# A convolution and feed-forward kernel on one Trainium2 core: the weight sums of two groups move from Pool to VectorE, and the first blocks' list is written anew

## The chip, the core and the metric

The kernel runs on one core of a Trainium2 chip. The metric is the time of one execution in microseconds (us) on the device; less is better. The engines have these names here: TensorE (PE in the profile; its weight loads are PEld), VectorE (DVE), ScalarE (ACT), Pool (GpSimd, POOL) and SyncE (SP, which here only issues transfers). Each engine works through its own list of instructions in order; between engines, semaphores make one wait for another.

## The reference

All data are float32. Each of 32768 tokens (8 sequences of 4096) has 192 channels in 8 heads of 24. First a causal convolution with 7 taps, softmaxed per head, then a feed-forward layer:

```python
w = softmax(weight, axis=-1)                          # 8 heads x 7 taps
out = np.einsum('hk,bskhg->bshg', w, x_unf)           # x_unf: 7 shifted views of x, zeros in front
h = out.reshape(B * S, 192) @ w_in                    # 192 x 2048
g = h * (1.0 / (1.0 + np.exp(-h)))
return g @ w_out                                      # 2048 x 192
```

## The kernel before, in words

**Blocks.** The tokens are taken in 32 blocks of 1024, as two halves of 512. A block is loaded (`load`, L184), turned by VectorE so that channels lie on partitions (`turn_in`, L474, "i"), given the 6 columns ahead of it (`halo_in`, L489, "ha": a small copy, then a transfer on SP's queue), convolved (`conv`, L502, "v": tap 0 by ScalarE; taps 1 to 6 by VectorE for the blocks up to 3, later by ScalarE and accumulating transfers), copied by SP's queue into the slots that the products read (`spread`, L523, "sp"), and six combinations of the slots are made by VectorE (`win`, L537, "w").

**Products.** Block 0 uses the plain products (`up_plain`, L577, and `down_plain`, L777, whose matmuls stand in 48 steps "dp"). All later blocks use a scheme of the Strassen kind with fewer products. For it the weights of five groups g = 0 to 4 are replaced in place by sums of each other: `combine(g, e)` (L379), with e = 0 for partitions 0 to 63 of the tiles and e = 1 for 64 to 127. `combine` makes 8 sums for e = 0 and 11 for e = 1, each on 64 partitions by 128 columns, from two operands in SBUF (group 4's first half has 3 more). Groups 0, 4 and 1 are combined by Pool at the end of the preparation (L1087), groups 2 and 3 by a step "go" of the list (L920): Pool copies one element of the loaded block, which makes it wait for that load, and then makes the 38 sums. Behind them on Pool stand the 16 sums for the output weights (`combine_out`, L417, 128x192 each), which `down_plain` issues with its last step.

**A block from 1 on.** Products P (`product`, L635; two matmul records each in the trace), six plain steps L (`plain`, L659), ScalarE's copies u of partial sums out of PSUM, VectorE's sums X, a, b (`sums_h`, L686), ScalarE's activations S and SL; then VectorE's differences t of the activations (`sum_g`, L718), the output products D (`out_slot`, L735), and the merging M, x, y, z, the transposes o and stores st. Step P13.0 reads a PSUM bank that X2.0 has written, P11.0 one of X4.0; P2 and P3 read window 1, P6 and P9 window 0. P2.0 accumulates into the bank that u5.0 has to copy first.

**The order.** Every engine's order is the order of the list: PLAN (L81) for blocks from 3 on, START (L104) for the first blocks. A step's mark tells the block: "=" two back, "-" one back, "+" one ahead of the pass; in START "=v.21" is tap 1 of channel group 2 for block 1, "-P5.0" a product of block 1, and unmarked steps belong to block 2 (a load, tap, spread or window is for the block after the one that the mark names). `step` (L882) turns a mark into instructions, all pinned in program order. A step's place matters only against steps of the same engine or queue; data and buffers (PSUM banks by the tables CHAIN_BANKS, XBANKS, PLAIN_BANKS and ACC) do the rest. In START of before the windows of block 1 stand behind all 18 VectorE taps of block 1, its 3 transposes for block 2 follow those taps, and taps of block 2 fill the gaps between the sums.

Of the kernel before, what the change touches and what calls it, by code (L numbers as in the profile page):

```python
# [12 lines left out]
ALU = mybir.AluOpType  # L13
# [4 lines left out]
def kernel(  # L18
# [83 lines left out]
        "u0.3 P9.3 S2.3 S0.4"  # L102
    )
    START = (  # L104
        "-ld.1 =v.10 -ld.0 =v.00 =v.11 =v.12 =dp.0 =dp.1 =dp.2 =dp.3 =v.13 =v.20 =v.21 =v.22 "
        "=v.23 =v.24 =v.25 =dp.4 =dp.5 =v.14 =dp.6 =dp.7 =dp.8 =dp.9 =v.15 =v.16 -ld.2 =sp.1 "
        "=dp.10 =dp.11 =v.26 =v.01 =v.02 =v.03 =dp.12 =v.04 =dp.13 =v.05 =v.06 =dp.14 =dp.15 "
        "=dp.16 =sp.2 =dp.17 =dp.18 =dp.19 =dp.20 =sp.0 -i.2 =go.2 -i.1 =dp.21 =dp.22 =dp.23 "
        "=dp.24 -i.0 =dp.25 =dp.26 =dp.27 =dp.28 =dp.29 =dp.30 -ha.0 =dp.31 =dp.32 =dp.33 "
        "=dp.34 ld.1 =w.0 =w.1 =dp.35 =dp.36 -v.00 =dp.37 =dp.38 =w.2 =dp.39 =dp.40 =dp.41 "  # L110
        "-v.01 =dp.42 -v.20 =dp.43 =dp.44 -v.02 -v.03 -v.10 -v.11 -v.12 =dp.45 =cp.0 =dp.46 "
        "=dp.47 =cp.1 -v.21 -P5.0 =w.3 -P5.4 -L.00 -u5.0 -v.13 -v.14 -L.11 -v.22 -P2.0 =cp.2 "
        "-u5.4 -P2.4 -L.12 -P3.0 -u4.0 -u4.4 -P6.0 -L.02 -u2.0 -L.01 -SL.0 -L.10 -SL.1 -P6.4 "
        "-u2.4 -P3.4 -SL.2 =o.1 -v.15 -P1.0 -u0.0 -X2.0 -P13.0 -S2.0 -v.23 -P5.2 =w.4 -u5.2 "
        "-P9.0 -P1.4 -u0.4 -P0.0 -u1.0 -P12.0 -P2.2 -X2.4 -P0.4 -P13.4 -S2.4 -X4.0 -P7.0 -u1.4 "
        "=o.2 -P14.0 -b1.0 -P10.0 =w.5 -S3.0 -u4.2 -a5.0 -b5.0 -S5.0 -v.04 -P11.0 -P9.4 -X4.4 "
        "-P14.4 =o.0 -P4.0 -S4.0 -a1.0 -P6.2 -u2.2 -P5.1 -P12.4 -b1.4 -P11.4 -P7.4 -P3.2 -P1.2 "
        "-P8.0 -u5.1 -S4.4 -a5.4 -P10.4 -u0.2 -S3.4 -P2.1 -u4.1 -P4.4 =st.0 -X2.2 -P13.2 -S2.2 "
        "-P9.2 -P0.2 -u1.2 -a0.0 -b5.4 -S5.4 -a1.4 -P12.2 -v.16 -P6.1 -u2.1 =st.1 -P5.3 -u5.3 "
        "-P8.4 -P14.2 -X4.2 -S3.2 i.1 -a0.4 -b1.2 -P3.1 -X2.1 -P1.1 -P7.2 -u0.1 -a5.2 -P2.3 "  # L120
        "-u4.3 -P3.3 -P11.2 -v.24 -P9.1 -S4.2 -X4.1 -P13.1 -P4.2 -P6.3 -S2.1 -a1.2 -u2.3 -P10.2 "
        "-b5.2 -P0.1 -P7.1 -P8.2 -P11.1 -X2.3 -P1.3 -S1.0 -P9.3 -v.25 -u1.1 -P14.1 -S4.1 -P12.1 "
        "-u0.3 -S1.4 -P13.3 -S3.1 -a5.1 -P4.1 -X4.3 -P7.3 -P0.3 -a0.2 -S5.2 -sp.1 +ld.1 -P12.3 "
        "P5.4 -v.26 -P11.3 -b1.1 -a5.3 -a1.1 -u1.3 -P10.1 -b1.3 -S2.3 -P4.3 -a1.3 -v.05 =st.2 "
        "-P8.1 -b5.1 -P10.3 -sp.2 -S0.4 -P14.3 -P8.3 ld.0 -S4.3 -S1.1 P5.0 -a0.1 -S0.0 -t.00 "
        "-D1.31 -D1.11 -S0.2 -D1.01 -S3.3 -D1.30 -t.01 -D2.00 -D2.01 -b5.3 -S5.3 -S1.2 -S5.1 "
        "-D0.11 -t.03 -D4.00 -a0.3 -D4.01 -t.02 -D3.00 u5.4 -D0.20 -S0.1 ld.2 -D5.00 -t.10 "
        "-t.11 -D2.11 -D3.01 -v.06 -sp.0 -D1.20 -S0.3 -D5.01 -t.13 -D4.11 -D5.10 -D4.10 i.2 "
        "-S1.3 i.0 -t.12 -D5.11 -D3.11 -t.20 ha.0 -t.21 -D0.10 -D2.10 u5.0 -D2.21 -w.0 -D2.20 "
        "-w.1 v.20 -D3.10 -D0.00 v.00 -t.23 -D4.21 -D4.20 -w.2 v.01 -t.22 -D3.21 -D0.21 -D0.30 "  # L130
        "-D0.31 -w.3 -t.30 v.21 -t.31 -D1.10 v.02 v.22 -D0.01 -D2.31 -t.32 -t.33 -D1.21 v.10 "
        "-D5.30 v.23 v.24 -y0.0 -D1.00 -y1.0 -D5.31 -z1.0 -D5.20 -D5.21 -x2.0 -x2.2 v.11 -D3.31 "
        "-D2.30 -x2.1 v.03 -x2.3 P2.0 u4.0 P3.0 -w.5 L.02 P2.4 u4.4 v.12 v.13 v.14 P6.0 u2.0 "
        "v.15 v.25 v.26 v.04 -M1.0 -M2.0 -y2.0 L.00 +ld.0 -M6.0 L.01 SL.0 X2.0 P6.4 u2.4 -D4.30 "
        "-D3.20 -D3.30 -M3.0 -x0.0 -D4.31 -x1.0 P9.0 P1.0 u0.0 -o.0 P13.0 S2.0 X4.0 P1.4 u0.4 "
        "-M4.0 -M5.0 P3.4 P5.1 u5.1 P11.0 X2.4 -w.4 P7.0 S4.0 P0.0 P12.0 P2.1 u1.0 P9.4 P0.4 "
        "u1.4 P13.4 a5.0 P4.0 b1.0 P10.0 X4.4 u4.1 S2.4 P7.4 P11.4 S4.4 P14.4 S3.4 v.16 P6.1 "
        "u2.1 P14.0 v.05 L.10 a1.0 a5.4 +ld.2 b5.0 P8.0 +i.2 a0.0 S3.0 P3.1 P4.4 a1.4 L.11 L.12 "
        "SL.1 P5.2 P12.4 SL.2 X2.1 v.06 P8.4 -st.0 u5.2 P1.1 P13.1 u0.1 b1.4 P5.3 sp.1 S0.0 "
        "u5.3 -o.3 S2.1 P12.1 P2.2 u4.2 -M7.0 P9.1 P0.1 u1.1 S1.4 +i.1 P2.3 u4.3 +i.0 a0.4 X4.1 "  # L140
        "S0.4 P10.4 P6.2 u2.2 P3.2 P7.1 P14.1 S3.1 P11.1 b1.1 b5.4 +ha.0 P10.1 +v.20 S4.1 P3.3 "
        "-o.1 P6.3 u2.3 X2.2 P9.2 P1.2 u0.2 a5.1 P4.1 X2.3 +v.21 P13.2 S2.2 P13.3 S2.3 P1.3 "
        "u0.3 -st.1 +v.00 P9.3 b5.1"
    )
    QUEUE = (0, 4, 1, 2, 3)
    CHAIN_BANKS = (
        ((4, 1, 2, 7, 7), (3, 4, 6, 5, 5), (1, 3, 3, 1, 0)),
        ((0, 2, 5, 4, 6), (1, 6, 1, 0, 7), (5, 3, 2, 3, 0)),
        ((5, 2, 5, 6, 7), (0, 4, 0, 3, 3), (1, 7, 2, 1, 1)),
    )  # L150
    XBANKS = (
        ((6, 2, 4, 2, 0), (6, 0, 0, 0, 4)),
        ((5, 1, 2, 7, 3), (4, 7, 3, 7, 4)),
        ((4, 0, 1, 7, 4), (6, 3, 1, 7, 6)),
    )
    PLAIN_BANKS = (
        (0, 2, 1),
        (5, 3, 4),
        (6, 3, 1),
    )  # L160
    ACC = (
        (1, 2, 7, 4, 3, 5, 7),
        (3, 4, 6, 1, 0, 2, 7),
        (0, 6, 1, 3, 4, 2, 7),
    )

# [10 lines left out]
    vec, act = Pinned(nc.vector), Pinned(nc.scalar)  # L177
# [4 lines left out]
    nats, xts, gs = {}, {}, {}  # L182
# [23 lines left out]
    x0 = x.flatten_outer_dims()[TB - pad : TB, :].rearrange("t (k c) -> c k t", k=NK)  # L206
# [11 lines left out]
    warm = const.tile([P, 1], F32, name="warm")  # L218
# [9 lines left out]
    pool = Pinned(nc.gpsimd)  # L228
# [138 lines left out]
            q >= NJ // 2,  # L367
        )

    def comb(out, u, v, op):  # L370
        pool.tensor_tensor(out, u, v, op=op)

    PLAIN = (1, NJ - 1, 1)

    def raw(g, i, k, e):
        a, j, own = chunks(g)[i]
        return rows(wr[j] if own == e else ws[j], e)[:, a, k, :]

    def combine(g, e):  # L379

        def op(sign, to, u, v):
            comb(raw(g, *to, e), raw(g, *u, e), raw(g, *v, e), ALU.add if sign > 0 else ALU.subtract)

        if (g, e) == (SWAP[0], 0):
            op(-1, (2, 1), (1, 0), (1, 2))
            op(-1, (2, 1), (2, 1), (0, 0))
            op(-1, (2, 1), (2, 1), (0, 1))
        for order in COMBINE[e]:
            op(*order)
# [382 lines left out]
                )  # L772
            )

    DOWN_BANKS = (0, 1, 5)

    def down_plain(b):  # L777

# [103 lines left out]
    def step(b, token):  # L882

        if token[0] in BACK:
            b, token = b - BACK[token[0]], token[1:]
        name, arg = token.split(".") if "." in token else ("", "")
        if b < 0 or b >= NB or not name or (b, token) in did:
            return
        if b == NB - 1 and token in held:
            return  # L890
        if b == NB - 1 and token[:3] == "D3." and (b, closing) not in did:
            later.append(token)
            return
        did.add((b, token))
        digits = [int(c) for c in arg]
        if name[0] == "P":
            product(b, digits[0], int(name[1:]), *digits[1:])
        elif name == "L":
            plain(b, *digits)
        elif name == "SL":  # L900
            silu_plain(b, *digits)
        elif name[0] in "uXabS":
            sums_h(b, name, *digits)
        elif name == "t":
            sum_g(b, *digits)
        elif name[0] == "D":
            i, (j, e) = int(name[1]), digits
            for half in range(2) if i == 3 and b == NB - 1 else (None,):
                out_slot(b, j, i, e, half)
        elif name[0] in "Mzyx":  # L910
            merge(b, name, *digits)
        elif name == "o":
            turn_out(b, *digits)
        elif name == "st":
            store_out(b, *digits)
        elif name == "dp":
            next(downs)
        elif name == "cp":
            copy_plain(b, *digits)
        elif name == "go":  # L920
            pool.tensor_copy(warm, nats[1][:, digits[0], 0, 0:1])
            for g in (2, 3):
                for e in range(2):
                    combine(g, e)
        elif name == "ld":
            if b + 1 < NB:
                load(b + 1, digits)
        elif b + 1 < NB:
            {"i": turn_in, "ha": halo_in, "v": conv, "sp": spread, "w": win}[name](
                b + 1, *digits[: 1 + (name == "v")]  # L930
            )
        if b == NB - 1 and token == closing:
            for t in later:
                step(b, t)
# [200 lines left out]
```

## Time and profile before

| | us |
|---|---|
| median of 3 runs (2319.98 to 2320.62) | 2320.21 |
| the profiled execution | 2319.66 |
| its span, first to last instruction | 2318.0 |
| TensorE busy in the span | 2309.5 |
| VectorE busy | 1797.6 |
| ScalarE busy | 1496.6 |
| Pool busy | 530.8 |

The profiled execution was taken from first to last instruction; 1.7 us of its time lie around the span. The granted TensorE clock was 0.999. The stages at the start, from the answer on stretches (busy us in each; start and end in us from the span's start):

| stretch | what TensorE does | PE | DVE | ACT | POOL |
|---|---|---|---|---|---|
| 0 to 59.67 | convolution and block 0, first layer | 58.19 | 52.44 | 29.84 | 25.23 |
| 59.67 to 101.02 | block 0, second layer | 41.35 | 39.90 | 9.42 | 39.39 |
| 101.02 to 137.95 | block 1, products | 36.93 | 33.69 | 28.28 | 26.97 |
| 137.95 to 178.03 | block 1, outputs (16 records of block 2 between) | 40.08 | 38.97 | 12.31 | 0.00 |
| 178.03 to 209.69 | block 2, products | 31.66 | 28.98 | 26.74 | 1.89 |
| 209.69 to 245.90 | block 2, outputs | 36.21 | 27.08 | 19.16 | 13.07 |

How to read the profile: a group or timeline line has the engine, the line of the kernel, the operation, the tile written and the tiles read, the shapes, and how many; what stands in brackets is the time that the engine sat idle before it and what ended that. Instructions of one engine overlap a little, so that the distance from one start to the next is often shorter than a duration. Matmul ends are modelled: TensorE counts as busy in stretches where its matmuls run at a poorer pace, and starts have to be compared.

### The profile page before, as it was taken

How to read it: one execution, taken by the hardware profiler on the slowest of the kernel's cores; microseconds unless marked ns; L12 is line 12 of the kernel's file. 1: busy time of each engine (PE TensorE's matmuls, PEld its weight loads, DVE VectorE, ACT ScalarE, POOL GpSimd, SP SyncE). 2: the span in 40 equal slices, each digit the busy share in tenths (PEclk: the TensorE clock that was granted, in tenths of full speed). 3: DMA queues.
4: the chain of work that ended last, by engine and by line, in shares of the span. 5: the costliest groups of instructions: out<-in, count | busy, mean ns of one | idle time of the engine just before them, and what ended most of it. 6: DMA issues, size and time to landing. Idle time of an engine off the chain costs nothing.

```text
span 2318.0 us, 45422 instructions
## 1 busy us (share of the span) xinstructions
PE 2309.5 (100%) x17630; PEld 950.3 (41%) x17630; DVE 1797.6 (78%) x2373; ACT 1496.6 (65%) x2779; POOL 530.8 (23%) x672
## 2 busy tenths in 40 slices
PE   9999999999999999999999999999999999999998
PEld 5454443444433344433444333443334443344433
DVE  8998777777777777777777777777778777777777
ACT  5347766677666686666776666866667666677543
POOL 4921112221122211222212222112221212221100
PEclk9999999999999999999999999999999999999999
DMA  7236556765567765677655676656676557765401
GB/s 159 58 62 103 97 99 117 124 116 101 95 111 121 122 107 91 108 120 120 109 100 98 114 124 116 105 93 112 118 123 108 96 101 120 120 114 95 80 16 25
DMA packets 523833, 238.81 MB, mean 103 GB/s; under 512 B 431648, under 2 KB 436768, under 8 KB 523616
## 3 DMA queue, kind: packets, MB, share of 16 engines
q0 software_dynamic: 73024, 133.73, 34.3%
q1 hardware_dynamic: 447392, 101.78, 24.9%
q8 instruction: 138, 2.26, 0.4%
q10 hardware_dynamic: 3200, 0.39, 0.1%
q14 instruction: 79, 0.65, 0.1%
HBM read 31.46 MB, written 25.17 MB: 24 GB/s over the span
## 4 chain that ended last, share of the span: by engine, by line
PE 89%; DVE 0%; ACT 0%; issue 0%; ACTq 0%
PE ps L765 45%; PE ps L649 39%; PE ps L666 5%; DVE cmb L175 0%; ACT u L175 0%; DVE osb L175 0%; ACTq L968 0%; ACTq L175 0%
## 5 line engine op out<-in xcount | busy, mean ns | idle before, releaser
L512 POOL DMA_DIRECT2D nat<-u x504 | 433.0, 945 | 1544.9 <-ACT u L511 1177.6
L765 PE MATMUL ps<-g,wo 128*32 128x512 f32 x2976 | 694.9, 592 | 0.0
L649 PE MATMUL ps<-win,wr 64*128 64x512 f32 x1550 | 688.7, 591 | 0.8 <-ACT yx L828 0.8
L649 PE MATMUL ps<-win,ws 64*128 64x512 f32 x1550 | 644.3, 589 | 0.0
L698 ACT COPY u<-ps 128x512 f32<-128x512 f32 x775 | 452.5, 588 | 163.4 <-PE ps L649 93.6
L765 PE MATMUL ps<-t,wo 128*32 128x512 f32 (+2 forms) x4528 | 538.5, 446 | 0.0
L765 PE MATMUL ps<-t,wx 128*32 128x512 f32 x2976 | 485.2, 592 | 0.0
L649 PE MATMUL ps<-dup,wr 64*128 64x512 f32 x868 | 425.6, 589 | 0.0
L511 ACT ACTIVATE u<-xt,taps 128x512 f32<-128x512 f32 x504 | 345.7, 715 | 43.6 <-DMA nat<-u 43.4
L733 DVE TENSOR_TENSOR t<-g,t 128x1024 f32<-128x1024 f32 x248 | 303.2, 1223 | 89.8 <-PE ps L765 84.2
L692 DVE TENSOR_TENSOR g<-u,ps 128x512 f32<-128x512 f32 x465 | 312.1, 682 | 72.2 <-PE ps L649 58.9
L649 PEld LDWEIGHTS ps<-win,wr 64*128 64x128 f32 x1550 | 275.7, 187 | 217.0 <-issue 177.0
L733 DVE TENSOR_TENSOR t<-g 128x1024 f32<-128x1024 f32 x248 | 298.8, 1216 | 76.4 <-PE ps L765 56.8
L692 DVE TENSOR_TENSOR ps<-u,ps 128x512 f32<-128x512 f32 x310 | 215.7, 696 | 132.4 <-ACT u L698 62.3
L710 ACT ACTIVATE g<-ps 128x512 f32<-128x512 f32 x465 | 281.1, 604 | 48.3 <-PE ps L649 46.8
L649 PEld LDWEIGHTS ps<-win,ws 64*128 64x128 f32 x1550 | 258.8, 187 | 125.9 <-issue 103.9
L710 ACT ACTIVATE g<-g 128x512 f32<-128x512 f32 x465 | 281.5, 629 | 30.2 <-DVE g L692 30.2
L765 PEld LDWEIGHTS ps<-t,wo 128*32 128x32 f32 x4528 | 181.4, 110 | 239.2 <-issue 227.6
L831 ACT COPY cmb<-ps 96x512 f32<-96x512 f32 x30 | 17.5, 582 | 396.9 <-PE ps L765 396.9
L649 PE MATMUL ps<-dup,ws 64*128 64x512 f32 x682 | 271.9, 589 | 0.0
L765 PE MATMUL ps<-g,wx 128*32 128x512 f32 x1488 | 245.9, 594 | 0.0
L765 PEld LDWEIGHTS ps<-g,wo 128*32 128x32 f32 x2976 | 170.4, 110 | 130.6 <-issue 129.8
(92 smaller groups left out, 2008.5 us busy)
## 6 DMA issues: line engine op xcount, KB each, us to landing
nat<-u POOLq DMA_DIRECT2D x504, 256.0 KB, 4.5
dup<-nat SPq DMA_DIRECT2D x345, 128.0 KB, 2.6
nat<-in_x_dram SPq DMA_DIRECT2D x382, 64.0 KB, 4.2
out_dram<-osb SPq DMA_DIRECT2D x376, 64.0 KB, 2.0
raw<-in_moe_w_out_dram SPq DMA_DIRECT2D x8, 384.0 KB, 3.9
raw<-in_moe_w_in_dram SPq DMA_DIRECT2D x12, 192.0 KB, 4.6
ws<-wr POOLq DMA_DIRECT2D x8, 192.0 KB, 4.8
raw<-in_moe_w_in_dram SPq DMA_DIRECT2D x6, 128.0 KB, 3.0
```

Of the source, the lines that this page charges most:

```text
L511: pin(nc.scalar.activation(z, src, AF.Copy, scale=tap))
L512: pin(nc.gpsimd.dma_start(out=dst, in_=z, accum_op=ALU.add))
L649: nc.tensor.matmul(to[:, cols], raw(g, *LEFT[e][r], e), rhs[:, cols], start=first, stop=True, skip_group_check=True,)
L666: nc.tensor.matmul(plain_bank(b, n and 1 + e)[:, cols], rows(wr[j] if own == e else ws[j], e)[:, a, k, :], rows(dups[b], e)[:, SLOT[e][2 * ...
L692: pin(nc.vector.tensor_tensor(out_, u, v, op=op))
L698: pin(nc.scalar.copy(us[b, g, o][:, cols], t1[:, cols]))
L710: pin(nc.scalar.activation(h, src, AF.Silu))
L733: pin(nc.vector.tensor_tensor(t[i // 2][:, i % 2, :], u, v, op=ALU.subtract))
L765: nc.tensor.matmul(accs[b][at][SQ * q : SQ * q + SQ, to], lhs[:, e, SQ * k : SQ * k + SQ], rhs[:, e, ts(q, TB // 4) if i == 5 else to], st ...
L831: pin(nc.scalar.copy(c[0], acc[0][0:n, :]))
```

## The change

The step "go" now names a group and a half, and its sums go to VectorE; the one-element copy on Pool is gone. START holds four such steps where it had one; the first blocks' list is another order of otherwise the same steps, and the bank tables of the first two entries are new. PLAN is untouched.

```diff
-    def comb(out, u, v, op):
-        pool.tensor_tensor(out, u, v, op=op)
+    def comb(out, u, v, op, engine=None):
+        (engine or pool).tensor_tensor(out, u, v, op=op)
...
-    def combine(g, e):
+    def combine(g, e, engine=None):
...
         elif name == "go":
-            pool.tensor_copy(warm, nats[1][:, digits[0], 0, 0:1])
-            for g in (2, 3):
-                for e in range(2):
-                    combine(g, e)
+            combine(*digits, vec)
...
-    DOWN_BANKS = (0, 1, 5)
+    DOWN_BANKS = (0, 5, 1)
...
     ACC = (
-        (1, 2, 7, 4, 3, 5, 7),
-        (3, 4, 6, 1, 0, 2, 7),
+        (2, 7, 1, 4, 5, 3, 7),
+        (1, 4, 3, 2, 0, 6, 7),
         (0, 6, 1, 3, 4, 2, 7),
     )
```

The new START up to its first sums, without the steps dp of block 0 (TensorE's own):

```
=v.20 =v.10 =v.21 =v.00 =v.01 =v.22 =v.02 -ld.2 =v.23 =v.11 =v.03 =v.12 =v.04 =v.13
-ld.1 =v.24 =v.05 =v.06 -ld.0 =v.14 -i.0 =v.15 =v.16 =sp.1 =go.20 =v.25 =sp.0 =go.30
=cp.0 =v.26 =go.31 -i.1 =sp.2 -i.2 -P5.0 -L.02 -L.00 =w.0 =cp.1 =w.1 -ha.0 =w.2 =w.3
=go.21 =cp.2 =w.4 -v.00 -u5.0 -P5.4 -u5.4 -v.10 -L.10 -v.11 -L.01 -P2.0 -u4.0 -P2.4
-P6.0 =o.0 -SL.0 -L.12 -u4.4 -P3.0 -P6.4 -u2.0 -P1.0 -L.11 -X2.0 -P13.0 =o.1 -v.20
```

The same stretch of the old one:

```
-ld.1 =v.10 -ld.0 =v.00 =v.11 =v.12 =v.13 =v.20 =v.21 =v.22 =v.23 =v.24 =v.25 =v.14
=v.15 =v.16 -ld.2 =sp.1 =v.26 =v.01 =v.02 =v.03 =v.04 =v.05 =v.06 =sp.2 =sp.0 -i.2
=go.2 -i.1 -i.0 -ha.0 ld.1 =w.0 =w.1 -v.00 =w.2 -v.01 -v.20 -v.02 -v.03 -v.10 -v.11
-v.12 =cp.0 =cp.1 -v.21 -P5.0 =w.3 -P5.4 -L.00 -u5.0 -v.13 -v.14 -L.11 -v.22 -P2.0
=cp.2 -u5.4 -P2.4 -L.12 -P3.0 -u4.0 -u4.4 -P6.0 -L.02 -u2.0 -L.01 -SL.0 -L.10 -SL.1
-P6.4 -u2.4 -P3.4 -SL.2 =o.1 -v.15 -P1.0 -u0.0 -X2.0 -P13.0
```

Later in START, taps of block 2 that stood ahead of block 1's outputs stand among them (five of 18 instead of one), the windows of block 2 stand at the end of those outputs instead of amid them, and one output step (D1.11) stands ahead of the last five products of block 1. On each engine the instructions of the blocks are the same in number, but for the 38 sums (from Pool to VectorE) and Pool's copy.

## The prediction

> **What bounds the kernel now.** I read the page first, then the TensorE rows around the places where stages meet, then VectorE and Pool side by side from 60 to 145 us, where the change lies.
>
> ```profile
> span 2318.0 us, 45422 instructions
> ...
> PE 89%; DVE 0%; ACT 0%; issue 0%; ACTq 0%
> ```
>
> The chain that ended last is TensorE almost alone, and its matmuls leave no hole worth a name. The only stop of size between 7 and 2300 us is this one, in the third block (columns: start, us, then engine, line and operation):
>
> ```profile
> 249.17 0.69 PE L649 MATMUL ps<-win,wr 64*128 64x512 f32 x1 [0.85 <-ACT yx L828]
> ```
>
> So nothing that is taken off another engine can bring much: the change moves no matmul out of the program. Its sign is decided by whether VectorE, which gets new work in the first blocks, makes TensorE stop. VectorE's rows there:
>
> ```profile
> 75.12 15.65 DVE L516 SCALAR_TENSOR_TENSOR nat<-xt,taps,nat 128x512 f32<-128x512 f32 x18
> 90.69 1.88 DVE L477 STREAM_TRANSPOSE xt<-nat 128x512 f32<-128x512 f32 x3
> 93.10 0.98 DVE L550 TENSOR_TENSOR win<-dup 128x512 f32<-128x512 f32 x1 [0.52 <-DMA dup<-nat]
> 94.11 0.97 DVE L550 TENSOR_TENSOR win<-win,dup 128x512 f32<-128x512 f32 x1
> ...
> 107.09 0.69 DVE L692 TENSOR_TENSOR ps<-u,ps 128x512 f32<-128x512 f32 x1 [1.11 <-ACT u L698]
> ...
> 132.46 0.74 DVE L516 SCALAR_TENSOR_TENSOR nat<-xt,taps,nat 128x512 f32<-128x512 f32 x1
> 133.12 0.68 DVE L692 TENSOR_TENSOR u<-u,ps 128x512 f32<-128x512 f32 x1
> ```
>
> The reader is to see two things. A convolution tap costs 0.865 us at the start (18 in 15.57, up to the transpose) and 0.66 later (132.46 to 133.12). And VectorE's first sum of the first stage, X2.0 at 107.09, had waited 1.1 us for ScalarE: VectorE was early there. Pool explains the two prices:
>
> ```profile
> 79.05 3.38 POOL L175 TENSOR_TENSOR wr<-wr 64x128 f32<-64x128 f32 x4
> ...
> 92.00 0.46 POOL L175 TENSOR_TENSOR ws<-ws,wr 64x128 f32<-64x128 f32 x1
> 92.53 0.46 POOL L175 TENSOR_TENSOR wr<-ws 64x128 f32<-64x128 f32 x1
> ...
> 118.99 0.59 POOL L175 TENSOR_TENSOR wx<-wo 128x192 f32<-128x192 f32 x1
> 119.66 0.59 POOL L175 TENSOR_TENSOR wx<-wx,wo 128x192 f32<-128x192 f32 x1
> ```
>
> While VectorE runs taps, Pool's sums take 0.85 each and the two engines take strict turns, one tap to one sum; while VectorE transposes (one input), Pool's sums start 0.53 apart. So an operation of VectorE with two operands in SBUF and a sum of Pool hold each other up. VectorE's sums on PSUM (L692) are not touched: 0.60 apart beside a busy Pool (118.71, 119.31).
>
> **The change part by part.** Pool loses the tiny copy and the 38 sums of groups 2 and 3, which it did from 94.1 to 118.9. Nobody waited for them on TensorE, so this saves nothing by itself. But Pool's 16 sums for the output weights (L424 to L427), at 119 to 130 before, now follow at 93.6. TensorE reads them only in the output stage at 137.95: no gain there, and the new list does not read them sooner.
>
> VectorE gets the 38 sums, 64x128 each, all with two SBUF operands. The trace has no such operation of VectorE. The nearest rows are the rounding operations on 256 columns, with Pool still:
>
> ```profile
> 8.17 0.42 DVE L175 SCALAR_TENSOR_TENSOR two<-raw,two 128x256 int32<-128x256 int32 x1
> 8.62 0.42 DVE L175 SCALAR_TENSOR_TENSOR mh<-mh,two 128x256 f32<-128x256 int32 x1
> 8.97 0.42 DVE L175 SCALAR_TENSOR_TENSOR two<-raw,two 128x256 int32<-128x256 int32 x1
> 9.42 0.42 DVE L175 SCALAR_TENSOR_TENSOR wr<-mh,two 128x256 f32<-128x256 f32 x1
> ```
>
> One that reads the result just before it starts 0.45 behind, one that doesn't 0.35. VectorE's pace is 1.05 ns an element (1.14 us for 1024 columns, 0.60 for 512), so 128 columns fewer are 0.135 less: 0.32 and 0.21. Of the 8 sums of an e = 0 part 2 read the one just before, of the 11 of an e = 1 part 6 do: 1.9 and 3.0 us, 9.8 for all four. That is the price without Pool.
>
> Now the ledger of VectorE's new list, from 75.12, where both lists begin. 14 taps at 0.865 give 87.2, one transpose 87.8, two taps 89.6. Up to here it is the old row in another order. Then go.20, a tap, go.30, a tap, go.31 and two transposes: 6.8 + 1.8 + 1.2, so 99.4. Four windows at 0.72 (153.31 to 154.03, Pool still): 102.3. go.21, a window, a tap, a transpose out and X2.0: 3.0 + 0.7 + 0.7 + 0.6 + 0.7, so X2.0 ends at 108.0.
>
> And TensorE's need for it. Block 1 starts at 101.02. A product is two matmul records, and the chain has 140 records in 30.04 us: 0.429 a product. The whole stage took 36.93, 1.3 more than its products; all of that is lost in the first 10 us, where the plain steps (L666, halves that pair badly) stand. In the new list P13.0, which needs X2.0, is the 15th step behind the same six plain steps: 101.02 + 14 x 0.429 + 1.2 = 108.2. **The margin is 0.2 us**, where the old list had VectorE waiting. A second path ends close by: the last transpose releases the halo transfer, that ScalarE's tap, that the copy u5.0, and that the product P2.0. In the old trace the tap started 2.2 us behind the transpose's end; with a tap of 0.65 and a copy of 0.6, a transpose at 99.4 lets P2.0 start at 102.9, and its turn is at 104.5: margin 1.6. The input transfers and the copies of the blocks (SP's queue) keep their order around this; the last four copies start with the last tap and have the third part of the sums to land in.
>
> Carried on with 0.63 a sum, 0.66 a tap and 1.17 a difference of the activations (L733), VectorE is 0.1 to 2 us ahead of TensorE at every later X and level with it at the difference t.11 (147.5 against 147.4). So what is lost at P13.0 is not got back, and some 0.5 comes on top. From 209 on VectorE has slack again (7.2 to 8.1 us busy in 10).
>
> What Pool adds decides. At 89.6 Pool has 6 sums of group 1 and the 16 on the output weights left; 2 taps take 2 of these, so 20 meet the new sums. Bounds: nothing, if VectorE's small sums slip into Pool's pauses; or VectorE falls to Pool's own pace, one sum to each of Pool's: 6 x 0.53 + 2 x 0.67 for go.20, 8 x 0.67 for go.30, 4 x 0.67 + 7 x 0.27 for go.31, 14.5 us instead of 6.8, so 7.7. The nearest rows are the meetings seen: a tap loses 0.2 (0.865 for 0.66), a window 0.28 (1.0 for 0.72). I take 0.24 x 20 = **4.8 us**.
>
> TensorE's own new order has one more change from products to outputs and back; such a pair loses 0.33 beyond the matmuls (0.12 in, 0.21 out, by the gaps at 137.4 and 170.2). The stop at 249.17 stays: the bank that P3.0 needs there is the one that x1 leaves, in the old bank table and in the new.
>
> Sum: 4.8 - 0.2 + 0.5 + 0.33 = 5.4 us. On the profiled execution, 2319.66 (span 2318.0 and 1.7 around it), that is 2325.1; the median of the runs shown is 0.55 higher: 2325.6, and I say 2325.5.
>
> [...]
>
> **The rivals.**
> *The sums slip between Pool's (0.27).* A turn of 0.865 holds 0.54 of tap (512 elements), so Pool's hold is at most 0.33 of its 0.53: a pause of 0.2, and a small sum that need not wait takes 0.21. If they fit, Pool costs nothing, the margin of 0.2 holds, and the time is 2319.66 + 0.33 + 0 to 2, about 2321.5: not slower. It decides whether the pause is as long as the sum; the 15 sums of 0.32, and Pool's longer ones, speak against it.
> *Pool's pace (0.17).* Each small sum waits out one of Pool's: 7.7 - 0.2 + 0.5 + 0.33 = 8.3, and 2328.5. For it: the turns are strict for every tap. Against: two small sums can pass in a long pause.
> *Another engine or queue is late first (0.05).* ScalarE's list is as full, and a window or copy may miss its turn: up to 3 us more. A gain is out of reach: the stop of 0.85 and the two stage changes are all there is, below 0.1%.
>
> **How the numbers follow.** Forecast 0.5 (3 to 7 us more), centre 2325.5. The range, 2320.4 to 2329.0, runs from the quiet case with only the stage change to Pool's pace with the 0.5. About 0.2% of this kernel, 4.6 us, is what a measurement can tell from no change. Slower by more: two thirds of the forecast, all of Pool's pace and a little of the last, 0.51. Within: 0.48. Faster: 0.01.
>
> **What would show it.** In the changed profile VectorE's 64x128 sums, 38 of them: mean start distance 0.45 or more while Pool works on wx confirms the turns, 0.25 the first rival. Pool's wx sums should stand at 93 to 106 us. Two transposes after go.31 should end at 104 (forecast), 99.4 (quiet) or 107. TensorE's products should stop in front of P2.0 and P13.0, by some 4 to 5 us between 103 and 114, with VectorE or ScalarE's u as the releaser. Wrong would be: no stop there, or the loss in the output stage after 137 us.

## The result, and the profile after

| | us |
|---|---|
| before, median of 6 runs (2319.98 to 2320.62) | 2320.33 |
| after, median of 6 runs (2328.80 to 2330.77) | 2330.28 |
| after, the profiled execution | 2330.7 |
| its span | 2329.0 |

After takes 1.0042 times as long as before (95% interval 1.0031 to 1.0053), 9.95 us more. The forecast was 2325.5 with a range up to 2329.0: the sign is right, the size is not.

The page of after says the same of the whole as that of before: TensorE alone makes the chain.

```profile
span 2329.0 us, 45436 instructions
...
PE 88%; DVE 0%; ACT 0%; issue 0%; ACTq 0%
```

TensorE's timeline of after has one new stop, at 109.45, and the old one of 0.85 in the third block, ten microseconds later than before (columns: start, us, engine, line, operation, shapes; in brackets the idle time ahead and who ended it):

```profile
103.99 1.23 PE L672 MATMUL ps<-dup,ws 64*128 64x256 f32 x3
109.45 3.78 PE L655 MATMUL ps<-win,wr 64*128 64x512 f32 x4 [4.23 <-ACT u L704]
...
259.37 0.69 PE L655 MATMUL ps<-win,wr 64*128 64x512 f32 x1 [0.85 <-ACT yx L834]
```

The first row that works after the stop matters as much as the stop. The four matmuls of the products P2.0 and P2.4 take 3.78 us there; at the usual 0.43 apart they take 1.98 (the same four with the stop filled, below). The stretches of after say why (stretch and its length; busy time and instructions of PE, PEld, DVE, ACT and POOL; then PEclk, the granted clock, the DMA share and GB/s):

```profile
104.00:106.00 2.00, 1.23 (x6) 0.37 (x2) 1.94 (x4) 0.00 (x0) 1.76 (x4) 1.00 0.00 0
106.00:108.00 2.00, 0.00 (x0) 0.00 (x0) 1.93 (x4) 0.00 (x0) 0.00 (x0) 1.00 0.05 2
108.00:110.00 2.00, 0.55 (x1) 0.50 (x2) 1.87 (x6) 1.79 (x4) 0.00 (x0) 0.86 0.05 2
110.00:112.00 2.00, 2.00 (x3) 0.67 (x2) 1.86 (x9) 0.95 (x2) 0.00 (x0) 0.50 0.03 8
...
116.00:118.00 2.00, 2.00 (x11) 1.13 (x10) 2.00 (x4) 0.91 (x3) 0.00 (x0) 0.93 0.43 66
```

TensorE stands still from 105.2 to 109.45 and then gets half its clock, 0.50, until 116.3. It counts as fully busy in that time, so the busy column alone hides the loss; the instruction counts (3 in 2 us, then 11) and PEclk show it.

Upstream of the stop stand ScalarE's rows of after, the tap behind the halo transfer and the copy u5.0:

```profile
108.21 0.72 ACT L514 ACTIVATE nat<-xt,taps 128x512 f32<-128x512 f32 x1 [5.56 <-DMA xt<-xt]
108.83 1.05 ACT L704 COPY u<-ps 128x512 f32<-128x512 f32 x2
```

Upstream of the transfer stand VectorE's sums (L175) and the last two transposes (L483). Its later rows, down to X2.0 (L698), are shown with them:

```profile
94.21 1.54 DVE L175 TENSOR_TENSOR wr<-wr 64x128 f32<-64x128 f32 x4
...
98.91 2.66 DVE L175 TENSOR_TENSOR ws<-ws 64x128 f32<-64x128 f32 x5
...
104.88 1.31 DVE L483 STREAM_TRANSPOSE xt<-nat 128x512 f32<-128x512 f32 x2
...
108.97 1.34 DVE L175 TENSOR_TENSOR ws<-ws 64x128 f32<-64x128 f32 x5
...
115.92 0.70 DVE L698 TENSOR_TENSOR ps<-u,ps 128x512 f32<-128x512 f32 x1 [1.89 <-PE ps L655]
```

Five sums of the same kind take 2.66 us while Pool works on the output weights and 1.34 when Pool has ended; Pool's rows of after for these weights:

```profile
94.68 0.72 POOL L175 TENSOR_TENSOR wx<-wo 128x192 f32<-128x192 f32 x1
...
105.33 0.59 POOL L175 TENSOR_TENSOR wo<-wo 128x192 f32<-128x192 f32 x1
```

X2.0, the sum that the forecast watched most, waited 1.89 us for TensorE, which was then at half clock. The stop itself stood earlier, at P2.0.

**Where the 11.0 us of span went**, from the starts of the stages in the two profiled executions. Block 1's products begin 0.93 later (101.95 for 101.02). From there to the end of block 2's outputs it takes 154.15 us instead of 144.88 (to 256.10 and to 245.90): 9.27. The later blocks are 71.19 apart in both, all but one; of the last 0.8, some 0.7 lie behind the start of the last matmul (7.2 us to the end of the span instead of 6.5). This last piece is 6.4 to 6.5 us long in the three profiled executions with the old list and 6.6 to 7.4 in the seven with the new one; why isn't shown. What the 9.27 consist of the page can't say, and the experiments take it apart.

### The profile page after: what moved, and what is told of

Read it like the earlier page. It is cut to its first block, busy times and chain, and to the rows that moved or that the text cites. A ratio compares the mean times of both kernels' runs of the same rounds, so it can differ in the third digit from the quotient of the medians.

```text
span 2329.0 us, 45436 instructions
## 1 busy us (share of the span) xinstructions
PE 2315.9 (99%) x17630; PEld 944.9 (41%) x17630; DVE 1808.8 (78%) x2411; ACT 1496.5 (64%) x2779; POOL 511.0 (22%) x633
## 4 chain that ended last, share of the span: by engine, by line
PE 88%; DVE 0%; ACT 0%; issue 0%; ACTq 0%
PE ps L771 45%; PE ps L655 39%; PE ps L672 5%; DVE cmb L175 0%; ACT u L175 0%; DVE osb L175 0%; ACTq L971 0%; ACTq L175 0%
## 5 line engine op out<-in xcount | busy, mean ns | idle before, releaser
L698 DVE TENSOR_TENSOR g<-u,ps 128x512 f32<-128x512 f32 x465 | 312.0, 682 | 71.3 <-PE ps L655 58.3
L698 DVE TENSOR_TENSOR ps<-u,ps 128x512 f32<-128x512 f32 x310 | 215.7, 696 | 132.1 <-PE ps L655 63.6
```

Source lines behind the costliest of these rows:

```text
L698: pin(nc.vector.tensor_tensor(out_, u, v, op=op))
```

## The experiments

The theory after reading the two traces: (1) Pool's sums for the output weights hold VectorE's new sums up, so the last transposes, the halo transfer and u5.0 come late and TensorE stops; (2) the stop makes the clock fall, and the half clock is a cost of its own; (3) the new list costs something without any sums. Rival A: VectorE is simply full, and its sums cost in any place, Pool or not. Rival B: the list, not the sums, is the loss. Before was timed again beside them: its medians were 2320.50, 2320.17 and 2320.52 in the three sessions.

### Pool's sums for the output weights behind VectorE's

```diff
-                            if j == NJ - 1:
-                                for c in range(NJ):
-                                    combine_out(c)
...
+        elif name == "wx":
+            pool.tensor_copy(warm[R:P], rows(wins[1], 1)[:, 4, 0:1])
+            for c in range(NJ):
+                combine_out(c)
...
-        "=cp.2 =w.4 -v.00 ...
+        "=cp.2 =w.4 =wx.0 -v.00 ...
```

> The changed kernel, with Pool's 16 sums of the output weights held back until VectorE has made window 4 (a one-element copy on Pool reads it). VectorE's 38 sums stay. Theory (VectorE's small sums and Pool's sums hold each other up, and the stop that follows also halves TensorE's clock): the parts go.30 and go.31 take 1.9 and 3.0 us instead of 3.9 and 6.0, the last transpose ends near 101 instead of 106, the stop of 4.2 in front of P2.0 is gone or under 1, the granted clock stays 1.00; time 2321 to 2322.5. Rival, the new list itself is late whoever makes the sums: the stop stays, 2326 or more. Rival, the sums are dear on VectorE even alone: both parts stay above 3 and 4.5 us, 2325 or more.

Measured: 2323.50 (2323.00 to 2324.50), ratio 1.0014 (1.0005 to 1.0023). VectorE's timeline of this kernel, at the same two places as above:

```profile
93.94 1.15 DVE L175 TENSOR_TENSOR wr<-wr 64x128 f32<-64x128 f32 x4
...
96.82 1.35 DVE L175 TENSOR_TENSOR ws<-ws 64x128 f32<-64x128 f32 x5
```

The second part takes 2.11 us (93.94 to the tap at 96.05) instead of 3.94, the third 3.08 instead of 5.97; the last transpose ends at 101.2, there is no stop ahead of P2.0, and the clock is 1.00 from 6.41 us on. So Pool is the cause of the stop: with the same list and the same 38 sums on VectorE, 6.8 of the 9.95 us are gone. Some 3 us stay, more than the 2322.5 expected at most. VectorE is busy for 40.8 of the 41 us from 105 to 146 in this kernel. TensorE shows no idle time in block 1, but its starts show delays: P2.0 begins 2.86 us behind block 1's first product (101.61), and only 2.25 behind it in the kernel below that has the same list and leaves the sums to Pool (first product 101.21). The two rows, this kernel's and that one's:

```profile
104.47 1.98 PE L655 MATMUL ps<-win,wr 64*128 64x512 f32 x4
...
103.46 0.59 PE L655 MATMUL ps<-win,wr 64*128 64x512 f32 x1
```

Nor is Pool out of VectorE's way altogether. The first part of the sums meets Pool as in after (3.25 us), and Pool's 16 sums, which now run from 108.56 to 121.17, hold up taps: the two from 117.47 on take 2.03 us, where two that Pool does not meet take 1.41 in after.

### TensorE kept busy in the stop

Eight matmuls of zeros into a bank that is free there fill the time ahead of P2.0; nothing else differs from after.

```diff
-... -v.11 -L.01 -P2.0 ...
+... -v.11 -L.01 =hot.0 -P2.0 ...
+        elif name == "hot":
+            for _ in range(8):
+                pin(nc.tensor.matmul(banks[4][:, 0 : 2 * P], zeros,
+                    zeros.unsqueeze(1).to_broadcast([P, 2, P]),
+                    start=True, stop=True, skip_group_check=True))
```

> The changed kernel, with 8 matmuls of zeros (128x256, some 0.43 us each, 3.4 in all) in TensorE's list in front of P2.0, into a bank that nothing uses yet: they stand inside the stop of 4.2 us. Theory (4.4 us are lost by waiting and some 3.4 more because TensorE runs at half clock for 6.8 us behind the stop): the clock stays 1.00, P2.0 starts at the same time, P13.0 then waits about 1 us for X2.0; time 2327 to 2328. Rival, the slow matmuls behind the stop are waits for ScalarE's copies and not the clock: the matmuls stay 0.85 apart, 2330 as before.

Measured: 2327.55 (2327.42 to 2327.67), ratio 1.0030 (1.0019 to 1.0042). TensorE's timeline:

```profile
104.84 3.72 PE L931 MATMUL ps<-zeros 128*128 128x256 f32 x16
109.28 1.98 PE L655 MATMUL ps<-win,wr 64*128 64x512 f32 x4 [0.72 <-ACT u L704]
```

P2.0 starts where it does in after (109.28 for 109.45), still released by u5.0, and the four matmuls from there on take 1.98 us instead of 3.78. The granted clock is 1.00 from 6.44 us on, and that is worth 2.7 us (2330.28 to 2327.55). The extra work makes the kernel faster than after. The wait of 1 us at P13.0 that was expected is not seen as idle time of TensorE. Yet VectorE is the one that is late there: X2.0 ran without a gap before it and ended at 114.46, and P13.0 began at 114.51. VectorE's row:

```profile
113.79 0.67 DVE L698 TENSOR_TENSOR ps<-u,ps 128x512 f32<-128x512 f32 x1
```

### Half of the filling

Four such matmuls instead of eight:

```diff
-            for _ in range(8):
+            for _ in range(4):
```

> As the kernel with 8 matmuls of zeros, but 4 (1.7 us), so that some 2.7 us of the stop stay empty. If an empty stretch has to be longer than about 3 us for the clock to fall: clock 1.00, 2327 to 2328. If any stop of this kind does it, or a share of busy time: half clock for some us, 2329 to 2330.

Measured: 2328.24 (2327.43 to 2328.78), ratio 1.0033 (1.0020 to 1.0045). The median lies between the two times that were expected, for the five times fall apart: 2327.4 and 2327.6, as with the whole filling (mean granted clock 0.999), and 2328.2, 2328.3 and 2328.8 (0.998). One of the latter was profiled; its timeline and stretches:

```profile
108.85 2.79 PE L655 MATMUL ps<-win,wr 64*128 64x512 f32 x4 [2.54 <-ACT u L704]
```

```profile
108.00:110.00 2.00, 1.15 (x3) 0.67 (x4) 1.87 (x8) 1.91 (x4) 0.00 (x0) 0.97 0.00 0
110.00:112.00 2.00, 2.00 (x6) 1.13 (x7) 1.90 (x7) 1.41 (x3) 0.00 (x0) 0.50 0.00 0
112.00:114.00 2.00, 2.00 (x7) 0.98 (x5) 1.40 (x3) 0.88 (x3) 0.00 (x0) 0.67 0.04 8
```

A stop of 2.54 us was still enough: the clock fell at 109.9 and came back at 113.3, half as long as in after.

### The new list, with the sums on Pool

```diff
         elif name == "go":
-            combine(*digits, vec)
+            if digits == [2, 0]:
+                for g in (2, 3):
+                    for e in range(2):
+                        combine(g, e)
```

> The new list and the new banks alone: the sums of groups 2 and 3 are made by Pool, one after the other, at the place of the first of the four parts. Theory (the list costs only the one more change between products and outputs, 0.33): no stop in front of P2.0 or P13.0, 2320.5 to 2321.2. Rival, the new list itself is late: stops stay in the products of block 1, 2325 or more.

Measured: 2321.86 (2321.36 to 2322.65), ratio 1.0007 (0.9998 to 1.0016): 1.4 us more than before by the medians, more than expected, though the interval still holds no change at all. Rival B falls as the main cause: the list is a small part. The profiled executions show where it is: from the start of block 1's products to the end of block 2's outputs it takes 147.05 us instead of 144.88, 2.17 more in this pair of executions. Some 0.5 lie in the stretch with the extra change from products to outputs (44.02 us for 40.08, with 16 records at 0.2146 more: six products of block 1 and two of block 2), where 0.33 was foreseen. 1.56 us lie in block 1's first stretch of products: 156 records in 35.06 us, where 33.50 would go by before's pace (36.93 for 172 records, less 16 at 0.2146). The one stop there waits for a sum of VectorE and comes 0.49 us behind its turn; what the rest consists of is not shown:

```profile
118.68 0.69 PE L655 MATMUL ps<-win,wr 64*128 64x512 f32 x1 [0.33 <-DVE g L698]
```

### The old list, with the sums on VectorE

```diff
         elif name == "go":
-            pool.tensor_copy(warm, nats[1][:, digits[0], 0, 0:1])
             for g in (2, 3):
                 for e in range(2):
-                    combine(g, e)
+                    combine(g, e, vec)
```

> The list and bank tables of before; all 38 sums made by VectorE where the old step stands, between the third and the second of the last transposes, Pool's sums for the output weights right behind group 1's. Theory (VectorE's place on the path is what costs, in any list): the sums take about 16 us beside Pool's, the last transposes end near 109 instead of 92.6, window 1 and the copy u5.0 come some 11 to 13 us later than TensorE's turn at P2.0, the stop lets the clock fall for one or two windows of 3.4 us, and the time is 2336 (2332 to 2339). Rival (the loss came with the new list, and the old one with its early windows bears the sums): below 2327.

Measured: 2333.34 (2332.97 to 2333.72), ratio 1.0057 (1.0044 to 1.0069). VectorE's 38 sums run from 91.40 to 108.07, 16.7 us, Pool's from there to 104.5 beside them. TensorE's timeline:

```profile
113.97 1.22 PE L666 MATMUL ps<-dup,ws 64*128 64x512 f32 x1 [10.76 <-ACT cmb L804]
```

The stop is longer than in after and stands earlier than P2.0, at the first plain step, which the expectation didn't see. ScalarE's timeline of this kernel tells why:

```profile
111.50 1.95 ACT L508 ACTIVATE nat<-xt,taps 128x512 f32<-128x512 f32 x3 [21.23 <-DVE win L553]
113.35 1.05 ACT L804 COPY cmb<-ps 128x512 f32<-128x512 f32 x2
```

In the old list the copies that free block 0's PSUM banks stand on ScalarE behind three taps that need the last transposes. The row puts the wait down to VectorE's window, which ended at 111.40; the halo transfer, issued at 109.44 and landing 1.9 us later, came at nearly the same time. Both stand behind the late transposes (108.07 to 109.38), so these hold the copies, and the copies the plain steps. The clock was 0.50 again, from 104.62 to 118.27, but only the last 4.3 us of that had work to slow down. So the new list is not what makes the sums dear; the stop with it is less than half of the old one's.

### Pool's work with one operand

```diff
-        comb(x_[0], a_(1, 0), a_(1, 1), ALU.add)
-        comb(x_[1], x_[0], a_(0, 0), ALU.subtract)
-        comb(x_[2], a_(0, 1), x_[1], ALU.subtract)
-        comb(a_(1, 0), a_(0, 0), a_(1, 0), ALU.subtract)
+        pool.tensor_copy(x_[0], a_(1, 0))
+        pool.tensor_copy(x_[1], x_[0])
+        pool.tensor_copy(x_[2], x_[1])
+        pool.tensor_copy(a_(1, 0), a_(0, 0))
```

> The changed kernel, with Pool's 16 sums for the output weights made as 16 copies of one operand in the same place (the sums are left out, so the second layer's weights are not the reference's). Theory A (what holds VectorE up is any Pool instruction on SBUF): the copies hold VectorE's sums as the sums did, in proportion to their own length: go.30 3.5 to 4, go.31 5 to 6 us, stop and half clock stay, 2329 to 2330. Theory B (only where both engines read two operands): go.30 about 2.1 and go.31 3.1 us as with Pool behind, no stop, 2323.5.

Measured: 2324.43 (2323.70 to 2325.05), ratio 1.0018 (1.0009 to 1.0027): near to theory B, but not what it said. The second part of the sums takes 2.66 us and the third 3.68, against 2.11 and 3.08 with Pool away and 3.94 and 5.97 with Pool's sums. Some 15 of Pool's operations stand beside these two parts in either kernel, so a copy (0.35 to 0.49 us long) costs VectorE (0.55 + 0.60) / 15 = 0.08 us and a sum of two operands (0.59) costs it (1.83 + 2.89) / 15 = 0.31. Pool's single-operand work wasn't free to VectorE here, but it was far cheaper than the sums. TensorE's timeline:

```profile
105.16 2.34 PE L655 MATMUL ps<-win,wr 64*128 64x512 f32 x4 [0.83 <-ACT u L704]
```

A stop of only 0.83 us, and 106.65 to 110.06 ran at half clock in this execution.

### The third part of the sums later

```diff
-        "=go.31 -i.1 =sp.2 =dp.47 -i.2 ...
+        "-i.1 =sp.2 =dp.47 -i.2 ...
...
-        "... -P9.4 -a5.0 =st.0 "
+        "... -P9.4 -a5.0 =st.0 =go.31 "
```

> The changed kernel, with the third part of the sums (11, group 3, e = 1) moved from ahead of the last transposes to behind the sums a5.0 of block 1's products, where Pool's sums for the output weights are over. Theory A (VectorE has no free time between 100 and 146 us, so its sums cost wherever they stand; only the half clock needs one long stop): the last transposes end at 100, P2.0 comes in its turn, the clock stays full, but TensorE loses 3 to 5 us in short waits for VectorE's sums between 108 and 130: 2325 to 2327. Theory B (the loss comes through the last transposes and u5.0 alone): as with Pool behind, 2323 to 2324.

Measured: 2329.08 (2328.68 to 2330.73), ratio 1.0040 (1.0026 to 1.0053). That is theory A's mechanism at a higher price than the 2327 it named at most, and the clock, which it had at full, fell. The 11 sums cost 3.0 us in the new place, Pool having ended, the transposes end at 99.5 and there is no idle time ahead of P2.0. But TensorE's timeline has two stops instead of one:

```profile
111.61 0.69 PE L655 MATMUL ps<-dup,wr 64*128 64x512 f32 x1 [2.06 <-DVE ps L698]
...
122.66 0.69 PE L655 MATMUL ps<-dup,wr 64*128 64x512 f32 x1 [2.20 <-DVE ps L698]
```

The first stands ahead of P13.0, which waits for X2.0: windows and go.21 now meet Pool. The second is the moved part itself. And the second stop, not the first, made the clock fall, from 123.8 to 127.2:

```profile
113.00:115.00 2.00, 2.00 (x11) 1.24 (x9) 1.76 (x4) 1.72 (x4) 0.00 (x0) 1.00 0.41 64
...
125.00:127.00 2.00, 2.00 (x8) 0.82 (x6) 1.38 (x3) 1.08 (x2) 0.00 (x0) 0.50 0.00 0
```

(The windows had also waited 1.76 us for the copies on SP's queue.) So rival A holds in part: VectorE has no room for these sums in the two places tried, and moving them moves the loss.

### The stop of the third block

In before, entries 4 and 5 of the second block's output bank table exchanged:

```diff
-        (3, 4, 6, 1, 0, 2, 7),
+        (3, 4, 6, 1, 2, 0, 7),
```

> Before, with two entries of the second block's output bank table exchanged (positions 4 and 5: banks 0, 2 become 2, 0), so that the first product of the fourth block's second chain no longer waits for the last copy x1. If the stop of 0.85 us at 249 is that bank alone, it goes and the time falls by 0.85 us or less, 2319.5 to 2320; if another wait stands behind it, nothing changes.

Measured: 2319.34 (2318.90 to 2320.51), ratio 0.9997 (0.9988 to 1.0006). The stop at 249 is gone from the profile and the distance of the two output stages around it falls from 72.31 to 71.84 us, so the bank was its cause; the gain can't be told from none. With the exchange the kernel no longer returns the right result, so this is the time of a test and not of a version.

### The sum of the pieces

| kernel | median, us | step | stretch, us | step |
|---|---|---|---|---|
| before (same session) | 2320.50 | | 144.88 | |
| new list, sums on Pool | 2321.86 | list: 1.4 | 147.05 | 2.2 |
| sums on VectorE, Pool's last 16 sums behind them | 2323.50 | 38 sums: 1.6 | 147.51 | 0.5 |
| Pool's 16 beside them, clock held by filling | 2327.55 | Pool's hold on VectorE: 4.05 | 151.73 | 4.2 |
| after | 2330.28 | half clock: 2.7 | 154.15 | 2.4 |

The stretch runs from the start of block 1's products to the end of block 2's outputs, in the one execution of each kernel that was profiled. It leaves out the start of the span, which differs from execution to execution (last section), and the piece behind the last matmul, whose differences of up to 0.9 us are not explained. In both columns the steps are differences of neighbours, so that they add up by themselves, to 9.8 and 9.27. What counts is that the columns agree on Pool's hold and on the half clock. List and sums together are 3.0 or 2.6; how that divides between the two is not settled. Each step of the medians carries the scatter of its two kernels (0.25 to 1.5 us from lowest to highest, and 2.0 in after, which was timed in another session), and another order of the steps wasn't tried.

## Why the prediction was wrong

**What bounds the kernel** held: TensorE alone, and the sign is set by whether VectorE makes it stop.

**The price of the sums alone** held: 2.97 us for the fourth part, where 3.0 was worked out, and 2.11 and 3.08 for the second and third without Pool, where it was 1.9 and 3.0.

**Pool's hold on VectorE** was the right mechanism, somewhat too small. The first three parts took 3.25 + 3.94 + 5.97 = 13.2 us against 6.8 quiet: 6.4 for 20 meetings, 0.31 each on the output weights, where 4.8 and 0.24 were taken and Pool's pace would have been 7.7. The last transpose ended at 106.2, where the forecast said 104 and Pool's pace 107; 0.8 of that is a later start of the whole list in this execution (the taps began at 75.93 instead of 75.12). The turns are not strict: 19 sums and a tap passed beside some 15 of Pool's. The five sums at 2.66 us for 1.34 show the hold for operations as short as these too. It differs by what Pool does: 0.08 us for each of its copies and 0.31 for each of its sums.

**The ledger of the two paths** held for VectorE and ScalarE. From the transposes' end to P2.0 it took 3.3 us, where 3.5 was worked out, and to the end of X2.0 8.4 with the clock held, where it was 8.6. TensorE's turn at P2.0 was put too late: with the sums on Pool it comes 2.25 us behind block 1's first product, in the ledger 3.5, so the margin of 1.6 was some 0.4. P13.0 was to set the loss, 4.6 late against 3.2 at P2.0. In after all of the idle time is at P2.0 (4.23 us, ScalarE's u the releaser, as the last part of the prediction allows) and X2.0 waited for TensorE. But this is the half clock's doing: in the filled kernel, with the clock held, P13.0 came directly behind X2.0.

**The step that failed is the sum: it prices a stop at its length.** 4.8 - 0.2 + 0.5 + 0.33 has no term for the clock after the stop. The stop of 4.23 us was followed by 6.83 us at half clock, and filling the stop without shortening it took 2.7 us off the time. With the clock held the loss is 7.05, within the forecast's own 3 to 7 us to a rounding; with the half clock, 9.95. The rows of before held no stop over 0.85 us and no clock below 0.99 between 7 and 2300 us, so no row showed this price. Nor did a row show that a stop of 4 to 5 us costs its length alone: the forecast took that for granted, and had no rival in which it costs more. The half clock lasted 6.827 us in after and 3.4 in the half filling; the windows that it followed are told below.

**The list's own cost** was mis-sized as well: 0.33 foreseen, 1.4 by the medians and 2.2 by the stretch. And the quiet case, 0 to 2 us beyond the list because VectorE is level with TensorE, is there as 1.6 or 0.5, with a part of Pool's hold still in it (the first part of the sums, and the taps from 108.6 us on). These two and Pool's 4.05 make the 7.05. That the forecast's 5.4 comes near it is partly chance: the list and the quiet case were set too low and Pool's share of the time too high, for the second and third part are 4.7 us longer than with Pool behind, of which 4.05 reach TensorE.

**The range.** Its upper end, 2329.0, counts the 0.5 twice: the sum at Pool's pace, which has the 0.5 in it, gives 2328.5.

**The signs to look for** came true and proved less than they seemed to. The sums beside Pool's work on the output weights were 0.49 and 0.54 us apart on the average, Pool's sums stood at 94.7 to 105.9 us, and TensorE stopped ahead of P2.0. None of the signs spoke of the clock, so they could not tell the forecast from what happened.

**The rivals.** Sums that slip between Pool's: refuted by these distances. Pool's pace: in VectorE's hold about as near as the forecast (6.4 between 4.8 and 7.7), and still below the measured time for want of the clock. Another engine late first: ScalarE's u was the releaser, but it was VectorE's transposes that made it late. No gain: right; the stop in the third block is there as before.

## What to carry to other kernels

Price a stop of TensorE with what follows it: here stops of 0.83 to 10.76 us were followed by 3.4 us or more of half clock, though stops of 0.85 and 2.06 us were not, and the stop of 4.23 us cost some 2.4 to 2.7 us beyond its own length. A stop that can't be avoided can be filled: here eight matmuls of zeros in it took 2.7 us off the time. Read the starts as well as the idle times: the delay of P2.0 in the first experiment shows in no idle time. When work moves from Pool to VectorE, ask what Pool will do in the time that it gains: here its next sums, which nobody waited for, moved up beside the new ones and cost more time than the sums themselves. Where VectorE has no free time, another place for its work only changed, here, which product waits.

## What the runs showed of the hardware

**The clock changed on a grid of 3.413 us, and it also fell after windows that were idle only in part.** The clock records change at steps of 3.413 us, counted from the grant at the start (4.08 to 7.06 us after the first instruction): once in before, 677 steps behind the grant, and 30, 32 and 679 steps behind it in after. Where the clock fell in block 1 of the other kernels, the half clock lasted one such step (3.4 us) or, with the old list, four (13.65 us). Laid on that grid, from the rows of TensorE's timelines:

| kernel, window (us) | TensorE idle in it | clock after it |
|---|---|---|
| after, 106.05 to 109.46 | all | 0.5 |
| after, 109.46 to 112.87 | none | 0.5 for one more, then full |
| half filling, 106.48 to 109.89 | 2.4 | 0.5 for one |
| third part late, 120.38 to 123.79 | 2.2 | 0.5 for one |
| old list, 101.20 to 104.62 | 1.4 | 0.5 for four windows, with the stop going on to 113.97 |
| Pool's work with one operand, 103.24 to 106.65 | 0.8 | 0.5 for one |
| third part late, 110.13 to 113.55 | 1.5 | full |
| after, 102.63 to 106.05 | 0.8 | full |

Only one of these windows was wholly idle. In the half filling, the later window of the third part late, the old list and Pool's work with one operand the clock fell after windows that were idle in part, for 2.4, 2.2, 1.4 and 0.8 us, and in after it stayed at half behind a window without idle time. Idle time alone doesn't part the rows: 0.8 us of it stands before a fall and before none. In the windows of the old list and of Pool's work with one operand, and in the one without idle time, most matmuls ran singly, of 64x512 or 64x256 each (in the old list four of them in 1.98 us from 101.23); in the late third part's window that kept the clock full they ran in pairs (started at 111.61 and 111.62, 112.15 and 112.16). Whether that is what counts stays open.

**The start of block 1 goes with the grant.** Block 1's products began at 101.02, 101.14, 101.23, 101.64 and 101.95 us in executions whose full clock was granted at 4.10, 4.32, 5.63, 6.44 and 7.06. The difference of 0.93 between the first and the last is that between the profiled executions of before and after, and it is no effect of the change: in the kernel with the half filling, which has the list of after, the grant came at 4.08 and the products at 101.11. How much of it the medians hold is not shown, for the other executions' traces were not kept.
